# Gated linear attention and two expert layers: the chunk state packed, its product on a 2x2 grid of array tiles, the masked products one slot later

## The chip, the cores and the metric

One Trainium2 chip, one of its cores (NeuronCores). The metric is the device time of the whole program in microseconds (us), less is better. TensorE does the matrix products, VectorE (DVE) and ScalarE (ACT) the elementwise work, GpSimd (POOL) small fills and indirect transfers; SyncE (SP) issues nearly all DMA transfers, one after the other. Each engine takes its instructions in a fixed order that was settled when the kernel was built.

## What is computed

Three stages, cut to what matters. B = 4 batches, H = 8 heads, S = 768 steps, D = 48; 3072 tokens of width 384.

```
f = 1 / (1 + exp(-f_logit))
for t in range(S):
    state = f[:, :, t, :, None] * state + einsum('bhd,bhde->...', k[:, :, t], v[:, :, t])   # outer product k v
    y[:, :, t] = einsum('bhd,bhde->bhe', q[:, :, t], state)
x = y as tokens x (heads * D)
h = x @ w_in;  x2 = (h * sigmoid(h)) @ w_out                # d_ff 2048
expert = argmax(x2 @ w_gate) per token;  out = gate * relu(x2 @ w1[expert]) @ w2[expert]     # 8 experts
```

## The kernel before

**Tiling and stages.** The 3072 tokens are 24 chunks of 128 (six a batch, numbered n = 0 to 23), in groups of two or three chunks. For each chunk the attention runs as six stages, `att0` to `att5`: att0 turns f_logit into logarithms (Exp and Ln on ScalarE); att1 sums them along the chunk with a triangular matrix (`pl`), takes exponentials (`en`, `ep`), scales k and q (`kpad`, `qpad`, each head padded from 48 to 64 columns) and sends the last row of `ep` through DRAM (`ends`) into `a_all`, the factor by which the state decays over the chunk; att2 transposes q and k (`pq`, `pk`, copied to `qt`, `kt`: 112 rows hold a pair of heads, rows 0 to 47 one head, 64 to 111 the other); att3 makes the scores (`sc`, two row tiles of 64 rows) and masks them with the triangle on VectorE (`am`); att4 makes the products; att5 splits the result into two parts of fewer bits (`xth`, `xtl`) for the next layer.

**att4 in the chunks from n = 7 on (`turned`, n >= YT).** The result is kept transposed. `py` first takes the state's part: one matmul for each pair of heads, with a 112 x 112 block of `state` that holds the two heads' 48 x 48 states on its diagonal and zeros beside them, moving `qt`. Then eight matmuls `py<-am,v` add the chunk's own part, each with a head's v (48 columns) as weights; the two heads of a pair write partitions 0 to 47 and 64 to 111, which are two column tiles of the array. ScalarE copies `py` to `yt` (one copy of 112 x 512), and six DMA transfers bring the rows of `yt` into `y`, from where att5 reads. Then `pu` (eight matmuls, kpad as weights, v moving) gives the state's update, which VectorE adds to and scales in `state`: two operations for each of the two heads of a pair, on 48 partitions each. The first chunk of a batch has no state product, the last has no `pu`. In chunks 0 to 6 the result is not turned, and am is the weight.

**What sets the order.** The first expert layer runs beside this as a sequence of slots. A slot is one step of 128 columns of its hidden width for one group: `moe_h` (nine matmuls `ph<-xtl/xth,in_*`), `se` on ScalarE, `sg` on VectorE, `moe_g` (`gh` on ScalarE, `gl` on VectorE), and, two slots behind (LAG = 2), `moe_o` (nine matmuls `px<-out_*`). Each attention stage is hung on a slot: for chunks from 7 on, stage j of a chunk stands at s0 + S1[j], where s0 is ASH slots ahead of the chunk's place in the group before (spacing about five slots), and its loads stand four slots ahead of s0. Within a slot ph comes first, then the stages, then gh and gl, then px. TensorE's order is kept as written; a scheduler settles the places on the other engines and queues. Matmul results live in eight PSUM banks: two for ph (`h`), three for px (`x`), and three (`a`) in turn for everything of the attention and for the gate's small matmuls (`plt`, `pg`, `pr`).

**Names.** In the trace a tile's name stands without its number: `py<-am,v` is a product of masked scores. Each f32 matmul is two records, a matmul of the rounded parts (fp32r) is one. `out_again`, `in_again` and `wmin` belong to a second reading of the weights that is spread over the slots. L333 is the helper through which all matmuls go, L338 that of the transposes.

Of the kernel before, what the change touches and what calls it, by code (L numbers as in the profile page):

```python
# [9 lines left out]
F32 = mybir.dt.float32  # L10
# [6 lines left out]
ALU = mybir.AluOpType  # L17
# [4 lines left out]
P = 128  # L22
# [29 lines left out]
ST5 = (7, 10, 12, 16, 16, 18)  # L52
ST6 = (14, 17, 19, 21, 23, 25)
LD = (-30, -30, -10, -5, -3, 5, 11)
S1 = (-2, 1, 3, 5, 6, 8)
ASH = 3
SG = 2
SE = 2
GB = 3
# [28 lines left out]
YT = 7  # L88
# [5 lines left out]
def kernel(  # L94
# [43 lines left out]
    att = phase.enter_context(tc.tile_pool(name="att", bufs=1))  # L138
    late = phase.enter_context(tc.tile_pool(name="late", bufs=1))

    def bank(kind, name):
        return ps.tile([P, 512], F32, tag=kind, name=name, bufs={"h": 2, "x": 3, "a": 3}[kind])
# [12 lines left out]
    a_all = const.tile([P, NCH, NPR], F32, name="a_all")  # L155
    state = const.tile([P, (NPR - 1) * 112 + P], F32, name="state")
    state_of = [state[:, r * 112 : r * 112 + P] for r in range(NPR)]
    state_all = state[:, : NPR * 112].rearrange("p (r e) -> p r e", r=NPR)
    qpads = [const.tile([P, H, 64], F32, name=f"qpad{i}") for i in range(2)]
    kpads = [const.tile([P, H, 64], F32, name=f"kpad{i}") for i in range(2)]  # L160
    wgc = const.tile([P, KC, 32], F32, name="wgc")
# [6 lines left out]
    def use(n, i, name):  # L168
        return bank(BANKS.get(n, "aaaaaaaa")[i], name)

    loaded = {}
# [7 lines left out]
    def load_chunk(n, names):  # L179
        b, c = divmod(n, CPB)  # L180
        g, r = group_of[n]
        for nm in names:
            src = {"f": f_logit, "q": q, "k": k, "v": v}[nm]
            if n == 1:
                tag = {"f": "sg", "q": "gh", "k": "gh", "v": "gl"}[nm]
                t = att.tile([P, H, D], F32, tag=tag, name=f"{nm}_{n}", bufs=BUFS[tag])
            elif nm == "f":
                if n == 0 or n == starts[g] and g > 1:
                    fb[g] = att.tile([P, CPG, H, D], F32, tag="in_f", name=f"f_{n}")
                t = fb[g][:, r] if g > 1 else fb[0][:, max(n - 1, 0)]  # L190
            else:
                t = att.tile([P, H, D], F32, tag="in_" + nm, name=f"{nm}_{n}")
            nc.sync.dma_start(out=t, in_=src[b, :, c * P : (c + 1) * P, :].rearrange("h p d -> p h d"))
            loaded[nm, n] = t

    units = {}

# [110 lines left out]
    am = {}  # L308
    ysb = {}
# [97 lines left out]
    def att4(n):  # L407
        _, qt = bd.pop(n)
        vt = loaded.pop(("v", n))
        a = am.pop(n)  # L410
        first, last = n % CPB == 0, n % CPB == CPB - 1
        py = use(n, 5, f"py_{n}")
        turned = n >= YT
        for r in range(0 if first else NPR):
            if turned:
                pe.matmul(py[:112, r * P : (r + 1) * P], state_of[r][:112, :112], qt[:, r, :], start=r == 0, stop=False)
        for r in range(NPR):
            if not turned and not first:
                pe.matmul(
                    py[:, r * 2 * D : (r + 1) * 2 * D], qt[:, r, :],  # L420
                    state_of[r][:112].rearrange("p (j e) -> p j e", j=2)[:, :, :D], start=True, stop=False,
                )
            for j in range(2):
                h = 2 * r + j
                ah = a[j][:, r, :]
                if turned:
                    o = py[64 * j : 64 * j + D, r * P : (r + 1) * P]
                    pe.matmul(o, vt[:, h, :], ah, start=first and r == 0, stop=r == NPR - 1)
                else:
                    pe.matmul(py[:, h * D : (h + 1) * D], ah, vt[:, h, :], start=first, stop=first or j == 1)  # L430
        if turned:
            yt = att.tile([P, NPR, P], F32, tag="am", name=f"yt_{n}", bufs=2)
            for rows in ((slice(0, D), slice(64, 64 + D)) if first else (slice(0, 112),)):
                nc.scalar.copy(yt[rows], py[rows].rearrange("p (r t) -> p r t", r=NPR))
            y = att.tile([P, KC, P], F32, tag="y", name=f"y_{n}")
            for j in range(2):
                nc.sync.dma_start(out=y[j * D : (j + 1) * D], in_=yt[64 * j : 64 * j + D, :KC])
            for src, dst, c, m in ((0, 96, 0, 32), (32, 96, 1, 16), (64, 112, 1, 16), (80, 96, 2, 32)):
                nc.sync.dma_start(out=y[dst : dst + m, c], in_=yt[src : src + m, KC])
        else:  # L440
            y = att.tile([P, KC, P], F32, tag="y", name=f"y_{n}")
            nc.scalar.copy(y[:, :, :96], py[:, : KC * 96].rearrange("p (c f) -> p c f", c=KC))
            nc.scalar.copy(y[:, :, 96:], py[:, KC * 96 : DM].rearrange("p (c f) -> p c f", c=KC))
        ysb[n] = y
        if last:
            return
        pu = use(n, 6, f"pu_{n}")
        for r in range(NPR):
            for j in range(2):
                h = 2 * r + j  # L450
                pe.matmul(
                    pu[64 * j : 64 * j + D, r * D : (r + 1) * D], kpads[n % 2][:, h, :D], vt[:, h, :], start=True, stop=True
                )
        pu3 = pu[:112, : NPR * D].rearrange("p (r e) -> p r e", r=NPR)
        for j in range(2):
            rows, cols = slice(64 * j, 64 * j + D), slice(0, D)
            ab = a_all[rows, n, :, None].to_broadcast([D, NPR, D])
            s = state_all[rows, :, 64 * j : 64 * j + D]
            if first:
                nc.vector.tensor_tensor(out=s, in0=pu3[rows, :, cols], in1=ab, op=ALU.mult)  # L460
            else:
                nc.vector.tensor_tensor(out=s, in0=pu3[rows, :, cols], in1=s, op=ALU.add)
                nc.vector.tensor_tensor(out=s, in0=s, in1=ab, op=ALU.mult)

    def att5(n):
        g, r = group_of[n]
        if r == 0:
            xt[g] = xt0 if g == 0 else tuple(
                att.tile([P, CPG, KC, P], F32R, tag=f"xt{s}", name=f"xt{s}_{g}", bufs=2) for s in ("h", "l")
            )  # L470
        xh, xl = xt[g]
        y = ysb.pop(n)
        if n >= YT:
            nc.scalar.copy(xh[:, r], y)
            nc.vector.tensor_sub(xl[:, r], y, xh[:, r].bitcast(F32))
            return
        pt = use(n, 7, f"pt_{n}")
# [37 lines left out]
    def moe_o(g, i):  # L515
        hi, lo = gt.pop((g, i))
        first, last = (0,), (NF - 1,)
        wh, wl = units["out", i // 4]
        if i in first:
            px[g] = [bank("a" if (g, t) == (1, 1) else "x", f"px_{g}_{t}") for t in range(sizes[g])]  # L520
        for t in range(sizes[g]):
            o = px[g][t][:, :DM]
            m = slice(t * P, (t + 1) * P)
            pe.matmul(o, hi[:, m], wl[:, i % 4, :], start=i in first, stop=False)
            pe.matmul(o, lo[:, m], wh[:, i % 4, :], start=False, stop=False)
            pe.matmul(o, hi[:, m], wh[:, i % 4, :], start=False, stop=i in last)
        if i in last:
            moe_x2(g, i)
# [583 lines left out]
    for n in range(NCH):  # L1112
        g, r = group_of[n]
# [22 lines left out]
    for j in range(2 * NF):  # L1136
        s = VS + j * VD // 2
# [55 lines left out]
    first = min(plan)  # L1193
# [19 lines left out]
    def fill(n):  # L1213
        for fn, i in ops[:n]:
            fn(items["head"], i)
        del ops[:n]

    def preload():
# [4 lines left out]
        o=lambda: moe_o(*outs.pop(0)), f=lambda: fill(1), F=lambda: fill(len(ops)), l=lambda: logits_pe(g),  # L1223
        m=lambda: logits_pe2(g), p=lambda: pick(g), r=lambda: route(g), w=preload, k=rank_rest,
# [51 lines left out]
```

## Time and profile before

| | us |
|---|---|
| median of 3 runs (844.62 to 848.91) | 847.7 |
| profiled execution | 845.27 |
| its span, first to last instruction | 843.6 |
| TensorE busy in it | 810.5 (96%) |
| VectorE, ScalarE busy | 483.4 (57%), 377.1 (45%) |
| mean granted clock of TensorE | 0.989 of full |

The program has an early part up to about 140 us in which the weights arrive and the first seven chunks run, a middle part up to about 560 us in which the slots and the chunks run side by side, and the eight experts after that. Matmuls are pipelined: a record of TensorE lasts from its first column to its last result, so that records overlap, and the distance between two starts tells what one costs. Where the start of the next instruction is later than that, the row gives the idle time and the engine that ended it in brackets.

### The profile page before, as it was taken

The numbers are of one execution on the slowest core, as the hardware profiler recorded it, in microseconds if no ns is written. First come the engines' busy times: TensorE is split into PE (matmuls) and PEld (weight loads), VectorE is DVE, ScalarE is ACT, GpSimd is POOL, SyncE is SP. The second block draws the span as 40 slices with busy tenths as digits, with TensorE's granted clock in tenths as the row PEclk, the third lists the DMA queues.
The fourth block names the chain that finished last, engine by engine and source line by source line (L and its number), as shares of the span: only waits on it lengthen the run. The fifth ranks groups of instructions, "written<-read, shape, count | busy, mean of one in ns | idle before, by whom it ended". The sixth has DMA issues, their size and how long they took to land.

```text
span 843.6 us, 15324 instructions
## 1 busy us (share of the span) xinstructions
PE 810.5 (96%) x5692; PEld 766.8 (91%) x5692; DVE 483.4 (57%) x1293; ACT 377.1 (45%) x805; POOL 59.1 (7%) x94
## 2 busy tenths in 40 slices
PE   7799989999999999999999999999999999999994
PEld 4689889999999999999999999989999999999993
DVE  5999965566665556555666556366464526435520
ACT  4565464453453453444444333365273525435520
POOL 2000000002001001001001000001110010110001
PEclk9899999999999999999999999999999999999998
DMA  9856863313244343254343321342281615624500
GB/s 206 189 147 163 250 193 96 66 39 101 74 100 104 74 94 106 67 105 104 76 95 94 86 57 48 104 132 67 97 276 55 200 56 171 200 80 164 168 16 27
DMA packets 166435, 95.92 MB, mean 114 GB/s; under 512 B 115692, under 2 KB 159965, under 8 KB 166352
## 3 DMA queue, kind: packets, MB, share of 16 engines
q1 hardware_dynamic: 162224, 83.80, 37.5%
q0 software_dynamic: 3280, 9.49, 2.9%
q10 hardware_dynamic: 848, 1.57, 0.6%
q8 instruction: 46, 0.75, 0.4%
q14 instruction: 37, 0.30, 0.1%
HBM read 75.61 MB, written 16.33 MB: 109 GB/s over the span
## 4 chain that ended last, share of the span: by engine, by line
PE 60%; DMA 12%; issue 10%; DVE 9%; ACT 4%; SPq 3%; POOLq 0%; POOL 0%; DVEq 0%; ACTq 0%
PE px L333 19%; PE ph L333 18%; DMA out_dram<-o,oi 6%; PE py L333 4%; PE po L333 4%; PE p L333 4%; PE sc L333 2%; DMA w_raw<-in_moe_w_dram 1%; DMA f<-in_f_logit_dram 1%; DVE am L404 1%; PE pl L333 1%; PE p_r L333 1%; PE po_r L333 1%; PE pq L338 1%; PE pk L338 1%
## 5 line engine op out<-in xcount | busy, mean ns | idle before, releaser
L333 PE MATMUL px<-out_lo,gh 128*128 128x384 f32 x384 | 137.3, 357 | 0.3 <-ACT gh L511 0.3
L501 ACT ACTIVATE se<-ph 128x384 f32<-128x384 f32 (+1 forms) x144 | 65.3, 454 | 159.7 <-PE ph L333 157.1
L333 PE MATMUL px<-out_hi,gl 128*128 128x384 f32 x384 | 130.2, 339 | 2.2 <-DVE gl L512 2.2
L333 PE MATMUL px<-out_hi,gh 128*128 128x384 f32 x384 | 129.7, 338 | 0.0
L333 PE MATMUL ph<-xtl,in_hi 128*128 128x384 f32 (+1 forms) x384 | 125.5, 327 | 1.2 <-DVE sg L503 0.9
L503 DVE SCALAR_TENSOR_TENSOR sg<-se,ph 128x384 f32<-128x384 f32 (+1 forms) x144 | 73.0, 507 | 90.9 <-ACT se L501 89.0
L333 PE MATMUL ph<-xth,in_hi 128*128 128x384 f32 (+1 forms) x384 | 124.0, 323 | 0.0
L333 PE MATMUL ph<-xth,in_lo 128*128 128x384 f32 (+1 forms) x384 | 123.8, 322 | 0.0
L511 ACT CAST gh<-sg 128x384 fp32r<-128x384 f32 (+1 forms) x144 | 68.7, 477 | 70.5 <-DVE sg L503 61.5
L512 DVE TENSOR_TENSOR gl<-sg,gh 128x384 fp32r<-128x384 f32 (+1 forms) x144 | 73.4, 510 | 29.2 <-ACT gh L511 28.1
L333 PEld LDWEIGHTS ph<-xtl,in_hi 128*128 128x128 f32 x384 | 72.5, 189 | 3.8 <-issue 1.4
L333 PEld LDWEIGHTS px<-out_hi,gl 128*128 128x128 f32 x384 | 72.6, 189 | 3.6 <-DVE gl L512 3.2
L333 PEld LDWEIGHTS px<-out_lo,gh 128*128 128x128 f32 x384 | 72.4, 188 | 3.2 <-ACT gh L511 0.9
L333 PEld LDWEIGHTS ph<-xth,in_lo 128*128 128x128 f32 x384 | 72.5, 189 | 0.0
L333 PEld LDWEIGHTS ph<-xth,in_hi 128*128 128x128 f32 x384 | 72.4, 189 | 0.0
L333 PEld LDWEIGHTS px<-out_hi,gh 128*128 128x128 f32 x384 | 72.3, 188 | 0.0
L227 DVE TENSOR_TENSOR w_lo<-w_raw,w_hi 128x384 fp32r<-128x384 f32 x128 | 65.1, 552 | 12.5 <-ACT w_hi L226 11.8
L333 PE MATMUL po<-w_lo,hh 128*128 128x384 f32 (+6 forms) x200 | 67.8, 339 | 0.0
L333 PE MATMUL po<-w_hi,hh 128*128 128x384 f32 (+6 forms) x200 | 67.2, 336 | 0.0
L333 PE MATMUL po<-w_hi,hl 128*128 128x384 f32 (+6 forms) x200 | 67.2, 336 | 0.0
L226 ACT CAST w_hi<-w_raw 128x384 fp32r<-128x384 f32 x124 | 56.9, 513 | 22.8 <-DMA w_raw<-in_moe_w_dram 19.5
L333 PE MATMUL p<-xsl,w_hi 128*128 128x480 f32 (+6 forms) x168 | 58.5, 348 | 0.0
(243 smaller groups left out, 1437.9 us busy)
## 6 DMA issues: line engine op xcount, KB each, us to landing
w_raw<-in_moe_w_dram SPq DMA_DIRECT2D x64, 384.0 KB
xs<-big SPq DMA_DIRECT2D x8, 776.0 KB
out_again<-in_moe_w_out_dram SPq DMA_DIRECT2D x16, 384.0 KB
xe<-xs SPq DMA_DIRECT2D x7, 776.0 KB
out_raw<-in_moe_w_out_dram SPq DMA_DIRECT2D x13, 384.0 KB
f<-in_f_logit_dram SPq DMA_DIRECT2D x24, 192.0 KB
k<-in_k_dram SPq DMA_DIRECT2D x24, 192.0 KB
q<-in_q_dram SPq DMA_DIRECT2D x24, 192.0 KB
```

What stands on the lines that cost most here:

```text
L226: (keep(nc.scalar.copy) if key == ("w1", 1, 1) and RT > 1 else nc.scalar.copy)(hi[:, h], x)
L227: lo_engine.tensor_sub(lo[:, h], x, hi[:, h].bitcast(F32))
L333: ins = nc.tensor.matmul(*a, **k)
L338: ins = nc.tensor.transpose(*a, **k)
L404: nc.vector.tensor_tensor(out=a, in0=sc4, in1=tri4, op=ALU.mult)
L501: nc.scalar.activation(e, ph[:, :GT], AF.Tanh, scale=0.5)
L503: nc.vector.scalar_tensor_tensor(out=t, in0=e, scalar=1.0, in1=ph[:, :GT], op0=ALU.add, op1=ALU.mult)
L511: (nc.scalar.copy if g < GACT else nc.vector.tensor_copy)(hi, t)
L512: (nc.gpsimd if (g, i) < LOV else nc.vector).tensor_sub(lo, t, hi.bitcast(F32))
```

## The change

Three things are changed, all of them in the attention.

1. **The state is packed.** From chunk 6 on each pair of heads takes 64 columns of `state` and not 112: the 48 x 48 state of one head on partitions 0 to 47, that of the other on 64 to 111, in the same columns. `carry` updates both with one add and one scaling on 112 partitions, where there were two of each on 48. For this `pu` is written 64 rows high for each head (kpad with its padding as weights).
2. **The state product is by head.** `att4_turned` makes eight matmuls of 48 rows and 64 columns, on the four tiles of a 2x2 grid of the array; the result goes to two banks, `pya` and `pyb`, of which the second has the two heads of a pair with partitions exchanged. The products of v and am go to the same places, with 64 columns of v as weights (v gets 16 columns more behind the last head, filled with zeros by GpSimd). `pu` follows in the columns of `pya` that are left. ScalarE copies the two banks in two halves, and y is brought into place by eight transfers and not six. 
3. **The slots.** ASH goes from 3 to 4 and the last two entries of S1 from 6 and 8 to 7 and 9: for chunks from 7 on, loads and att0 to att3 come a slot earlier, att4 and att5 stay where they were.

```
-S1 = (-2, 1, 3, 5, 6, 8)
-ASH = 3
+S1 = (-2, 1, 3, 5, 7, 9)
+ASH = 4
...
+    packed_state = state[:, : NPR * 64].rearrange("p (r e) -> p r e", r=NPR)
...
+            if nm == "v":
+                tag, bufs = ("gl", GB) if n == 1 else ("in_v", 1)
+                flat = att.tile([P, H * D + 16], F32, tag=tag, name=f"v_{n}", bufs=bufs)
+                if n >= YT:
+                    nc.gpsimd.memset(flat[:, H * D :], 0.0)
...
+        if turned:
+            att4_turned(n, qt, vt, a, first, last)
+            return
         py = use(n, 5, f"py_{n}")
-        turned = n >= YT
-        for r in range(0 if first else NPR):
-            if turned:
-                pe.matmul(py[:112, r * P : (r + 1) * P], state_of[r][:112, :112], qt[:, r, :], start=r == 0, stop=False)
...
-                if turned:
-                    o = py[64 * j : 64 * j + D, r * P : (r + 1) * P]
-                    pe.matmul(o, vt[:, h, :], ah, start=first and r == 0, stop=r == NPR - 1)
...
-            for j in range(2):
-                nc.sync.dma_start(out=y[j * D : (j + 1) * D], in_=yt[64 * j : 64 * j + D, :KC])
-            for src, dst, c, m in ((0, 96, 0, 32), (32, 96, 1, 16), (64, 112, 1, 16), (80, 96, 2, 32)):
-                nc.sync.dma_start(out=y[dst : dst + m, c], in_=yt[src : src + m, KC])
...
+        packed = n >= CPB
+        wide = 64 if packed else D
         for r in range(NPR):
             for j in range(2):
                 h = 2 * r + j
                 pe.matmul(
-                    pu[64 * j : 64 * j + D, r * D : (r + 1) * D], kpads[n % 2][:, h, :D], vt[:, h, :], start=True, stop=True
+                    pu[64 * j : 64 * j + wide, r * D : (r + 1) * D], kpads[n % 2][:, h, :wide],
+                    vt[:, h * D : (h + 1) * D], start=True, stop=True,
                 )
+        if packed:
+            carry(n, pu[:112, : NPR * D], first)
+            return
...
+    def carry(n, pu, first):
+        pu3 = pu.rearrange("p (r e) -> p r e", r=NPR)
+        ab = a_all[:112, n, :, None].to_broadcast([112, NPR, D])
+        s = packed_state[:112, :, :D]
+        if first:
+            nc.vector.tensor_tensor(out=s, in0=pu3, in1=ab, op=ALU.mult)
+        else:
+            nc.vector.tensor_tensor(out=s, in0=pu3, in1=s, op=ALU.add)
+            nc.vector.tensor_tensor(out=s, in0=s, in1=ab, op=ALU.mult)
+
+    def att4_turned(n, qt, vt, a, first, last):
+        halves_of = [use(n, 5, f"pya_{n}"), use(n, 6, f"pyb_{n}")]
+
+        def place(r, j):
+            b, c = divmod(r, 2)
+            k = j ^ b
+            return halves_of[b][64 * k : 64 * k + 64, c * P : (c + 1) * P]
+
+        if not first:
+            for c in range(2):
+                for r in (c, c + 2):
+                    for j in range(2):
+                        rows = slice(64 * j, 64 * j + D)
+                        pe.matmul(place(r, j), packed_state[rows, r, :], qt[rows, r, :], start=c == 0, stop=False)
+        for r in range(NPR):
+            for j in range(2):
+                h = 2 * r + j
+                pe.matmul(
+                    place(r, j), vt[:, h * D : h * D + 64], a[j][:, r, :], start=first and r % 2 == 0, stop=r % 2 == 1
+                )
+        pu = halves_of[0][:, 2 * P : 2 * P + NPR * D]
+        if not last:
...
+                    pe.matmul(
+                        pu[64 * j : 64 * j + 64, r * D : (r + 1) * D], kpads[n % 2][:, h, :],
+                        vt[:, h * D : (h + 1) * D], start=True, stop=True,
+                    )
+        yt = att.tile([P, NPR, P], F32, tag="am", name=f"yt_{n}", bufs=2)
+        for b in range(2):
+            nc.scalar.copy(
+                yt[:112, 2 * b : 2 * b + 2], halves_of[b][:112, : 2 * P].rearrange("p (r t) -> p r t", r=2)
+            )
+        y = att.tile([P, KC, P], F32, tag="y", name=f"y_{n}")
+        for j in range(2):
+            nc.sync.dma_start(out=y[j * D : (j + 1) * D, :2], in_=yt[64 * j : 64 * j + D, :2])
+            nc.sync.dma_start(out=y[j * D : (j + 1) * D, 2], in_=yt[64 - 64 * j : 64 - 64 * j + D, 2])
+        for src, dst, c, m in ((64, 96, 0, 32), (96, 96, 1, 16), (0, 112, 1, 16), (16, 96, 2, 32)):
+            nc.sync.dma_start(out=y[dst : dst + m, c], in_=yt[src : src + m, KC])
```

Up to the slot in which chunk 7's scans start, TensorE's order is the same but for the width of chunk 6's pu. Three places where it is not follow; x4 is a row that repeats, sizes are those of the result.

TensorE at the products of chunk 8, before:

```order
L333 MATMUL ph_8_2207<-xth_1059,in_hi 128x384
L333 MATMUL py_2221<-qt_2084,state 112x128 x4
L333 MATMUL py_2221<-am_0_2170,v_1810 48x128
L333 MATMUL py_2221<-am_1_2172,v_1810 48x128
...
L333 MATMUL pu_2243<-v_1810,kpad_88 48x48 x8
L333 MATMUL pl_2256<-lfh_2087,trir 128x384
L333 MATMUL pl_2256<-lfl_2088,trir 128x384
L338 MATMUL plt_1_2268<-ident,x_1_1867 128x128 x3
L333 MATMUL px_0_1930<-out_lo,gh_6_2131 128x384
```

The four rows of the state product are eight after it, and pl of the next chunk has gone a slot ahead:

```order
L341 MATMUL ph_8_2226<-xth_1059,in_hi 128x384
L341 MATMUL pya_2240<-qt_2054,state 64x128 x2
L341 MATMUL pyb_2241<-qt_2054,state 64x128 x2
L341 MATMUL pya_2240<-qt_2054,state 64x128 x2
L341 MATMUL pyb_2241<-qt_2054,state 64x128 x2
L341 MATMUL pya_2240<-am_0_2148,v_1784 64x128
...
L341 MATMUL pyb_2241<-am_0_2148,v_1784 64x128
...
L341 MATMUL pya_2240<-v_1784,kpad_88 64x48 x8
L346 MATMUL plt_1_2288<-ident,x_1_1868 128x128 x3
L341 MATMUL px_0_1947<-out_lo,gh_6_2152 128x384
```

VectorE at the masks of chunk 17 (am; sg and gl are the expert layer's, wmin waits for a transfer of weights), before:

```order
L503 SCALAR_TENSOR_TENSOR sg_7_4686<-se_7_4684,ph_7_4674 128x384
L260 TENSOR_REDUCE wmin<-out_again 128x1
L404 TENSOR_TENSOR am_0_4698<-sc_0_4688,trir 128x512
L404 TENSOR_TENSOR am_1_4700<-sc_1_4689,trir 128x512
L512 TENSOR_TENSOR gl_7_4703<-sg_7_4686,gh_7_4702 128x384
L503 SCALAR_TENSOR_TENSOR sg_8_4727<-se_8_4725,ph_8_4715 128x384
```

After it the masks stand ahead of gl_6 and of that wmin, and sg_7 behind both:

```order
L412 TENSOR_TENSOR am_0_4712<-sc_0_4702,trir 128x512
L713 TENSOR_REDUCE r_lim_4924<-r_oh_4724 128x3
L731 COPY x_12_4461<-r_den_4730 128x1
L412 TENSOR_TENSOR am_1_4714<-sc_1_4703,trir 128x512
L568 TENSOR_TENSOR gl_6_4736<-sg_6_4700,gh_6_4735 128x384
L714 TENSOR_TENSOR r_off_4734<-r_off_4734,r_lim_4924 128x3
L715 TENSOR_SCALAR r_lim_4924<-r_lim_4924 128x3
L268 TENSOR_REDUCE wmin<-out_again 128x1
L334 CAST lfh_4920<-f_4831 128x384
L559 SCALAR_TENSOR_TENSOR sg_7_4760<-se_7_4758,ph_7_4748 128x384
```

ScalarE at the end of the middle part, where xth of chunk 23 waits for y, before:

```order
L434 COPY yt_6493<-py_6480 112x512
L501 ACTIVATE se_12_6540<-ph_12_6530 128x384
L511 CAST gh_12_6544<-sg_12_6542 128x384
L474 CAST xth_6206<-y_6495 128x384
L501 ACTIVATE se_13_6567<-ph_13_6557 128x384
L511 CAST gh_13_6579<-sg_13_6569 128x384
```

After it there are two copies to yt, and xth stands behind se_13:

```order
L508 COPY yt_6592<-pya_6574 112x256
L508 COPY yt_6592<-pyb_6575 112x256
L557 ACTIVATE se_12_6642<-ph_12_6632 128x384
L567 CAST gh_12_6646<-sg_12_6644 128x384
L557 ACTIVATE se_13_6669<-ph_13_6659 128x384
L530 CAST xth_6300<-y_6595 128x384
L567 CAST gh_13_6681<-sg_13_6671 128x384
```

So ScalarE's wait for y there now has gh_13 right behind it, and no longer se_13.

## Rows read from the trace of the kernel before

**Rows 1.** Busy time by stretch: window, length, busy us of each engine, clock, DMA.

```profile
140.00:530.00 390.00, 388.53 (x2939) 371.34 (x2938) 231.07 (x658) 169.15 (x335) 18.88 (x19) 1.00 0.34 83
```

**Rows 2.** What TensorE waited for, 140 to 545 us: total, times, longest.

```profile
PE py L333 <- DVE am L404: 1.4, 5, 0.6
PE ph L333 <- DVE sg L503: 0.9, 1, 0.9
```

**Rows 3.** Timeline of TensorE, chunk 7's products: start, length, what, count.

```profile
151.52 0.34 PE L333 MATMUL ph<-xth,in_hi 128*128 128x384 f32 x1
151.69 1.04 PE L333 MATMUL py<-qt,state 112*112 112x128 f32 x8
152.66 1.08 PE L333 MATMUL py<-am,v 128*48 128x128 f32 x16
153.57 0.53 PE L333 MATMUL pu<-v,kpad 128*48 128x48 f32 x16
154.03 0.44 PE L333 MATMUL pl<-lfh,trir 128*128 128x384 f32 x1
```

**Rows 4.** Timeline of TensorE, chunk 7's scores.

```profile
147.09 0.34 PE L333 MATMUL ph<-xth,in_hi 128*128 128x384 f32 x1
147.36 1.16 PE L333 MATMUL sc<-qt,kt 48*128 48x128 f32 x16
148.45 0.44 PE L333 MATMUL px<-out_lo,gh 128*128 128x384 f32 x1
```

**Rows 5.** Timeline of TensorE, one group's gate products.

```profile
229.81 0.86 PE L333 MATMUL pg<-rt,wgc 128*32 128x128 f32 x18
```

**Rows 6.** Timeline of TensorE, chunk 6: am as weights, then pu.

```profile
118.58 1.88 PE L333 MATMUL py<-v,am 128*128 128x48 f32 x16
120.39 0.56 PE L333 MATMUL pu<-v,kpad 128*48 128x48 f32 x16
```

**Rows 7.** Timeline of TensorE, products of chunks 11, 14, 17 and 23, and what followed.

```profile
243.97 1.04 PE L333 MATMUL py<-qt,state 112*112 112x128 f32 x8
...
247.18 0.44 PE L333 MATMUL pl<-lfh,trir 128*128 128x384 f32 x1
...
311.62 1.04 PE L333 MATMUL py<-qt,state 112*112 112x128 f32 x8
...
314.41 0.44 PE L333 MATMUL pl<-lfh,trir 128*128 128x384 f32 x1
...
379.47 1.04 PE L333 MATMUL py<-qt,state 112*112 112x128 f32 x8
...
382.38 0.44 PE L333 MATMUL pl<-lfh,trir 128*128 128x384 f32 x1
...
524.16 1.04 PE L333 MATMUL py<-qt,state 112*112 112x128 f32 x8
...
526.14 0.44 PE L333 MATMUL px<-out_lo,gh 128*128 128x384 f32 x1
```

**Rows 8.** Timeline of VectorE ahead of chunk 17's masks.

```profile
379.57 0.55 DVE L260 TENSOR_REDUCE wmin<-out_again 128x1 f32<-128x384 f32 x1 [1.19 <-DMA out_again<-in_moe_w_out_dram]
```

**Rows 9.** Groups by form: count, busy us, mean ns of one, idle before.

```profile
L434 ACT COPY yt<-py 112x512 f32<-112x512 f32 x15 | 8.8, 584 | 2.6 <-PE py L333 2.4
L462 DVE TENSOR_TENSOR state<-pu,state 48x192 f32<-48x192 f32 x24 | 8.5, 354 | 0.4
```

**Rows 10.** ScalarE's wait for y; SyncE's issues of y, chunk 7.

```profile
ACT xth L474 <- DMA y<-yt: 18.6, 17, 5.4
...
154.62 1.25 SPq L437 DMA_DIRECT2D y<-yt  x2
155.91 2.49 SPq L439 DMA_DIRECT2D y<-yt  x4
```

**Rows 11.** Timeline of ScalarE and TensorE where chunk 23's y comes late.

```profile
536.65 0.51 ACT L474 CAST xth<-y 128x384 fp32r<-128x384 f32 x1 [5.38 <-DMA y<-yt]
...
538.28 0.45 PE L333 MATMUL ph<-xtl,in_hi 128*128 128x384 f32 x1 [0.87 <-DVE sg L503]
```

More of the change, by code (lines that the diff above doesn't have):

```diff
@@ L183, in load_chunk @@
             src = {"f": f_logit, "q": q, "k": k, "v": v}[nm]
-            if n == 1:
-                tag = {"f": "sg", "q": "gh", "k": "gh", "v": "gl"}[nm]
+            if nm == "v":
[3 more added lines that the diff above has]
+                    nc.gpsimd.memset(flat[:, H * D :], 0.0)
+                t = flat[:, : H * D].rearrange("p (h d) -> p h d", h=H)
+                loaded[nm, n] = flat
+            elif n == 1:
+                tag = {"f": "sg", "q": "gh", "k": "gh"}[nm]
                 t = att.tile([P, H, D], F32, tag=tag, name=f"{nm}_{n}", bufs=BUFS[tag])
@@ L193, in load_chunk @@
             nc.sync.dma_start(out=t, in_=src[b, :, c * P : (c + 1) * P, :].rearrange("h p d -> p h d"))
-            loaded[nm, n] = t
+            loaded.setdefault((nm, n), t)
     units = {}
@@ L411, in att4 @@
         first, last = n % CPB == 0, n % CPB == CPB - 1
+        turned = n >= YT
+        if turned:
+            att4_turned(n, qt, vt, a, first, last)
+            return
         py = use(n, 5, f"py_{n}")
-        turned = n >= YT
-        for r in range(0 if first else NPR):
-            if turned:
-                pe.matmul(py[:112, r * P : (r + 1) * P], state_of[r][:112, :112], qt[:, r, :], start=r == 0, stop=False)
         for r in range(NPR):
-            if not turned and not first:
+            if not first:
                 pe.matmul(
@@ L424, in att4 @@
                 h = 2 * r + j
-                ah = a[j][:, r, :]
-                if turned:
-                    o = py[64 * j : 64 * j + D, r * P : (r + 1) * P]
-                    pe.matmul(o, vt[:, h, :], ah, start=first and r == 0, stop=r == NPR - 1)
[L429 to L435, printed above, removed]
-            for j in range(2):
-                nc.sync.dma_start(out=y[j * D : (j + 1) * D], in_=yt[64 * j : 64 * j + D, :KC])
-            for src, dst, c, m in ((0, 96, 0, 32), (32, 96, 1, 16), (64, 112, 1, 16), (80, 96, 2, 32)):
-                nc.sync.dma_start(out=y[dst : dst + m, c], in_=yt[src : src + m, KC])
[L440 to L443, printed above, removed]
+                pe.matmul(
+                    py[:, h * D : (h + 1) * D], a[j][:, r, :], vt[:, h * D : (h + 1) * D], start=first,
+                    stop=first or j == 1,
+                )
+        y = att.tile([P, KC, P], F32, tag="y", name=f"y_{n}")
+        nc.scalar.copy(y[:, :, :96], py[:, : KC * 96].rearrange("p (c f) -> p c f", c=KC))
+        nc.scalar.copy(y[:, :, 96:], py[:, KC * 96 : DM].rearrange("p (c f) -> p c f", c=KC))
         ysb[n] = y
@@ new lines, in att4_turned @@
+    def att4_turned(n, qt, vt, a, first, last):
[4 more added lines that the diff above has]
+            return halves_of[b][64 * k : 64 * k + 64, c * P : (c + 1) * P]
+        if not first:
+            for c in range(2):
[11 more added lines that the diff above has]
+        if not last:
+            for r in range(NPR):
+                for j in range(2):
+                    h = 2 * r + j
+                    pe.matmul(
+                        pu[64 * j : 64 * j + 64, r * D : (r + 1) * D], kpads[n % 2][:, h, :],
[5 more added lines that the diff above has]
+                yt[:112, 2 * b : 2 * b + 2], halves_of[b][:112, : 2 * P].rearrange("p (r t) -> p r t", r=2)
+            )
+        y = att.tile([P, KC, P], F32, tag="y", name=f"y_{n}")
+        for j in range(2):
+            nc.sync.dma_start(out=y[j * D : (j + 1) * D, :2], in_=yt[64 * j : 64 * j + D, :2])
+            nc.sync.dma_start(out=y[j * D : (j + 1) * D, 2], in_=yt[64 - 64 * j : 64 - 64 * j + D, 2])
+        for src, dst, c, m in ((64, 96, 0, 32), (96, 96, 1, 16), (0, 112, 1, 16), (16, 96, 2, 32)):
+            nc.sync.dma_start(out=y[dst : dst + m, c], in_=yt[src : src + m, KC])
+        ysb[n] = y
+        if not last:
+            carry(n, pu[:112], first)
```

## Prediction

> **What bounds the kernel now.** I read the busy time by stretch first. Between 140 and 530 us, the stretch that holds the products of all 17 chunks that the change treats anew (7 to 23), TensorE is busy 388.5 of 390 us at a granted clock of 1.00 [rows 1]. The list of what TensorE waits for in 140 to 545 us has two lines: masks (am) from VectorE, 1.4 us of idle in five waits, and one 0.9 us wait for a sg [rows 2]. So nothing but TensorE's own stream and those waits sets the end there; a microsecond taken out of the stream, or out of these waits, comes off the whole, and work on ScalarE and VectorE counts only where it makes TensorE late. I then read one changed chunk (chunk 7) record by record on TensorE [rows 3], the scores (sc) that feed its masks [rows 4], and the chunks whose products had to wait [rows 7].
>
> In [rows 3] the state product is 8 records (each f32 matmul is two) that follow one another: 152.66 - 151.69 = 0.97 us to the first am product, of which 0.10 is the change of tiling between them (next part); the rest is 0.11 us a step. From the start of the last ph before it to the first am product it takes 152.66 - 151.52 = 1.14 us. The am products and pu are 16 records each, but in two column tiles side by side: 0.91 us and 0.46 us for 8 steps.
>
> **The state product on a 2x2 grid: 15 chunks (7 to 11, 13 to 17, 19 to 23).** It becomes 16 records, by head, with 48 rows and 64 columns, 4 for each of four tiles. No row of before has such tiles, so I bound them. The nearest is sc [rows 4]: 16 records in two row tiles, 128 columns moving. Its first record stands 147.36 - 147.09 = 0.27 us after the last ph, against 151.69 - 151.52 = 0.17 for the state product now: that is the price of one more change of tiling, 0.10 us. From its first record to the next px, change of tiling included, it takes 1.09 us for 8 steps. With four tiles at work at once there are 4 steps: 1.09 - 4 x 0.11 = 0.65. The weights are 64 columns wide and not 128: the am products, with 48, last 1.08 us from first start to last end where sc lasts 1.16 [rows 3, 4], so up to 0.06 less. New block: 0.27 + 0.59 to 0.65 = 0.86 to 0.92, for 1.14: a saving of 0.22 to 0.28 us. I take 0.25; 15 x 0.25 = **3.8 us less**. That three tiles can run at once shows in the gate's 18 records, 6 for each of three column tiles, that last 0.86 us [rows 5]; in single file they would need 18 x 0.11 = 2.0.
>
> **Wider weights.** The stationary slice grows from 48 to 64 columns in the am products and in pu. The am products move 128 columns, which take the 0.11 step with any width of weights seen here, so nothing changes. pu moves only 48. With 48 moving columns behind 128 columns of weights, chunk 6 needs (120.39 - 118.58)/16 = 0.113 us a record; behind 48 columns chunk 7's pu needs (154.03 - 153.57)/8 = 0.057 a step [rows 3, 6]. Between these, 64 columns cost 16/80 x 0.056 = 0.011 more a step, 0.09 for 8 steps; there are 15 such pu (6 to 10, 12 to 16, 18 to 22; the last chunk of a batch has none): **1.3 us more**. Bounds: 0 (48 moving columns hide it) and 1.6.
>
> **Products one slot later.** Relative to the rest of the program the scans, transposes, scores and masks come one slot of 16 earlier; the products and xth stay. So the masks have two slots and not one. Four chunks paid for this. Chunk 11 took 247.18 - 243.97 = 3.21 us from first product to the next matmul, chunk 17 382.38 - 379.47 = 2.91, where chunk 23, without wait and also without pu, took 526.14 - 524.16 = 1.98; chunk 14 took 314.41 - 311.62 = 2.79, chunk 7 154.03 - 151.69 = 2.34 [rows 3, 7]. That is 1.23 + 0.93 + 0.45 = 2.6 us (the list of waits counts less, since a column tile that waits beside one that runs is not idle time there). Why they wait: chunk 17's masks stood on VectorE behind a wmin that waited 1.19 us for the landing of out_again [rows 8]; in the new order they stand ahead of it. **2.6 us less**; bounds 1.3 (half stay) and 3.0 (chunk 18 waited a little too).
>
> **What lies beside TensorE.** The carry is two VectorE operations and not four of 0.35 us [rows 9]: 0.7 us less a chunk, not on the path. The yt copy of 0.58 us [rows 9] becomes two of half the width, together under 1.2 us. The second must be over before the carry may read the same bank, a new wait on VectorE, behind which sg, kpad and gl are queued. Nothing of this reaches TensorE unless it grows past about 3 us: the bank that a sg frees is needed when the ph after next starts, two px blocks and one ph later, 27 steps of some 0.17 us [rows 3], of which se and sg themselves take about 1. The small POOL memsets of v have five slots.
>
> The y transfers become 8 and not 6. Each holds SyncE's queue 0.62 us ((1.25 + 2.49)/6), so y lands 1.25 us later. ScalarE already waits at xth, 18.6 us over 17 chunks, at longest 5.4 [rows 10], with se, gh and qt queued behind. The longest one shows what the cover is worth: ScalarE idled 5.38 us and TensorE 0.87 [rows 11], so some 4.5 us are free. The other sixteen wait (18.6 - 5.4)/16 = 0.83 us on average; 0.83 + 1.25 = 2.1 stays within 4.5. For chunk 23 xth now stands behind se_13, so that ph_15 no longer waits, but gh_13 and gl_13 do, and px_13 needs them: between 0.9 less and 1.3 more; I take 0.
>
> **Sum:** -3.8 + 1.3 - 2.6 = -5.1 us. On the profiled execution, 845.27 us (span 843.6, the rest lies around it), this gives 840.2. That execution lies 2.4 us under the median of the three runs, 847.7; a term that is a time of TensorE's stream is the same on either, so the forecast for the median is 842.6.
>
> **The rivals.**
> *Pairs.* Two row tiles write the two halves of one bank here, which no row of before shows: sc's two row tiles have a bank each, and the column tiles that share one have the same rows. If such writes exclude one another, the grid runs two at a time, 8 steps: 0.89 + 4 x 0.11 = 1.33 us, 0.19 more than now. 15 x 0.19 = 2.9; 2.9 + 1.3 - 2.6 = +1.6: 849.3 us. For it: nothing measured; against it: each pair writes disjoint partitions, as the column tiles do. The Trainium skill has the rule that speaks for it ("TensorEngine Tiling (Array Packing)", Gotcha 1: PSUM Pressure): different row tiles cannot access the same PSUM bank at the same time, and by it the time would be these 849.3 us. Its page "PSUM — Partial Sum Buffer" (PSUM bank collisions raise a hardware error) narrows that to one bank and 32-partition quadrant and says that the chip does not stall for it; no run here shows either.
> *Single file.* The four tiles don't overlap at all, since a head's records alternate over rows and columns: 16 steps, 0.89 + 12 x 0.11 = 2.21 us, 1.07 more; 15 x 1.07 = 16.1, + 1.3 - 2.6 = +14.8: 862.5, slower. This decides from the point where a block takes over 1.14 + (4.2 + 1.3)/15 = 1.51 us, ten steps. For it: the change of tiling costs time already in [rows 3]; against it: rows 4 and 5, where tiles of one direction overlap fully.
> *Masks still late.* VectorE's in-order queue puts something else ahead of the masks and the 2.6 us stay: 845.2. For it: wmin waits for a landing wherever it stands; against it: the new order.
> *y too late.* If two more transfers delay y by 5 us, as where the queue was crowded at the end, 0.83 + 5 - 4.5 = 1.3 us at 17 chunks, 23 us: 865. For it: [rows 11]; against it: the sixteen others.
>
> **How the numbers follow.** The forecast, with cover and bounds as above (840 to 845 us): 0.60. Pairs: 0.11. Single file: 0.06. Masks still late: 0.13. y too late: 0.05. Something else: 0.05. Half a per cent is 4.2 us, about what a measurement of this kernel can tell from no change; the forecast's -5.1 lies close to that line, so that of its 0.60 I put 0.46 beyond it and 0.14 within; masks still late gives 0.02 and 0.11, pairs 0.10 within and 0.01 slower, single file and y too late are slower, the rest is split. Faster 0.50, same 0.36, slower 0.14. The range holds the forecast, late masks and most of pairs: down to 838.5 (0.28 for each block, 3.0 of waits, pu for nothing, 0.9 at the end: -8.1, and a little), up to 849.5.
>
> **What would show it.** In the profile after, chunk 7's state records (pya, pyb from qt) should start in fours within some 0.03 us, and last start of ph to first am product should read 0.9 us; 1.3 means pairs, 2.2 single file. pu should last 0.09 us longer. The mask waits should be gone from TensorE's list, xth's idle time should be 1 to 1.3 us longer at those chunks where it stands at the same place in ScalarE's queue, with no new line for sg or gl on TensorE. If TensorE waits for gl or sg at more than one or two chunks, the reasoning on the cover is wrong.

## The result: 859.6 us, slower by 1.5%

| | before | after |
|---|---|---|
| median of 4 runs, taken in turn | 846.6 us (844.6 to 848.9) | 859.6 us (858.3 to 861.8) |
| ratio, 95% interval | | 1.0146 [1.0123, 1.0169] |
| profiled execution, and its span | 845.27, 843.6 us | 858.32, 856.3 us |

The forecast was 842.6 us with a range that ended at 849.5. The products of the change did what was forecast, and the time was lost elsewhere. First the list of what TensorE waited for from 140 to 545 us in the kernel after (total, times, longest), which answers to [rows 2]:

```profile
PE pg L341 <- ACT rt L633: 6.4, 4, 3.0
PE pg L341 <- ACT qt L392: 2.3, 1, 2.3
PE ph L341 <- DVE xtl L531: 1.0, 1, 1.0
PE ph L341 <- DVE sg L559: 0.2, 1, 0.2
```

The waits for masks (am) are gone, as forecast. In their place stand 9.9 us of waits, of which 8.7 belong to products that the prediction never looked at: pg, the gate's small matmuls, waiting for ScalarE. Now chunk 7 on TensorE, which answers to [rows 3]:

```profile
154.90 0.34 PE L341 MATMUL ph<-xth,in_hi 128*128 128x384 f32 x1
155.16 0.33 PE L341 MATMUL pya<-qt,state 48*64 48x128 f32 x2
155.18 0.33 PE L341 MATMUL pyb<-qt,state 48*64 48x128 f32 x2
155.32 0.28 PE L341 MATMUL pya<-qt,state 48*64 48x128 f32 x2
...
155.54 0.28 PE L341 MATMUL pya<-qt,state 48*64 48x128 f32 x2
155.56 0.28 PE L341 MATMUL pyb<-qt,state 48*64 48x128 f32 x2
155.76 0.66 PE L341 MATMUL pya<-am,v 128*64 128x128 f32 x8
156.25 0.61 PE L341 MATMUL pyb<-am,v 128*64 128x128 f32 x8
156.69 0.62 PE L341 MATMUL pya<-v,kpad 128*64 128x48 f32 x16
157.24 0.44 PE L341 MATMUL px<-out_lo,gh 128*128 128x384 f32 x1
```

The state records start in fours, the last start of ph lies 155.76 - 154.90 = 0.86 us ahead of the first am product (1.14 before), pu takes 157.24 - 156.69 = 0.55 us (0.46 before), and the whole block 157.24 - 154.90 = 2.34 us where chunk 7 took 154.03 - 151.52 = 2.51: 0.17 less, as the two terms 0.25 and 0.09 say together.

**Where pg waits.** TensorE and ScalarE of the kernel after, where group 1's gate falls:

```profile
170.19 0.84 PE L341 MATMUL pg<-rt,wgc 128*32 128x128 f32 x10 [2.97 <-ACT rt L633]
```

```profile
161.58 1.17 ACT L326 ACTIVATE f<-f 128x1152 f32<-128x1152 f32 x1 [0.35 <-DMA v<-in_v_dram]
...
163.65 1.28 ACT L327 ACT_TABLE_LOAD   x1
164.94 1.17 ACT L327 ACTIVATE f<-f 128x1152 f32<-128x1152 f32 x1
166.02 0.46 ACT L633 COPY rt<-plt 128x384 f32<-128x384 f32 x1
167.46 0.51 ACT L530 CAST xth<-y 128x384 fp32r<-128x384 f32 x1 [0.98 <-DMA y<-yt]
167.98 1.28 ACT L557 ACT_TABLE_LOAD   x1
169.28 0.49 ACT L557 ACTIVATE se<-ph 128x384 f32<-128x384 f32 x1
169.66 0.47 ACT L633 COPY rt<-plt 128x384 f32<-128x384 f32 x1
```

pg multiplies the copies rt. ScalarE runs in order, and Exp and Ln of f (the first stage of the next group's three chunks) with the load of a function table (ACT_TABLE_LOAD) behind each, 1.17 + 1.28 + 1.17 + 1.28 = 4.9 us, now stand ahead of the second copy, and all but the last load ahead of the first. In the kernel before the two copies were out first and f came after them:

```profile
158.26 0.47 ACT L577 COPY rt<-plt 128x384 f32<-128x384 f32 x1
...
163.47 0.47 ACT L577 COPY rt<-plt 128x384 f32<-128x384 f32 x1
...
167.23 1.17 ACT L318 ACTIVATE f<-f 128x1152 f32<-128x1152 f32 x1
```

At this wait the idle TensorE is paid twice, since its granted clock falls behind it; behind the waits of 2.14 us at 376.75 and 2.32 us at 444.93 it stayed at 1.00. Busy time by stretch, kernel after (window, length, busy us of PE, PEld, DVE, ACT, POOL, then granted clock, DMA share, GB/s):

```profile
165.00:170.00 5.00, 2.22 (x14) 1.70 (x12) 0.76 (x2) 3.99 (x6) 0.00 (x0) 1.00 0.03 9
170.00:175.00 5.00, 4.81 (x31) 4.17 (x33) 1.26 (x3) 1.40 (x4) 0.00 (x0) 0.66 0.00 0
```

The clock is 1.00 (2.4 GHz) until the stall and 0.66 on average after it, so it stood at 1.2 GHz for part of that stretch; 0.34 x 5 = 1.7 us of work at the full clock.

**Ledger.** Starts of the first ph of slots 16, 128 and 136, read from the timelines, cut the span in four; the later tables use the same cuts.

| us | to slot 16 | 16 to 128 | 128 to 136 | 136 to the end | span |
|---|---|---|---|---|---|
| before | 88.8 | 452.7 | 20.8 | 281.3 | 843.6 |
| after | 91.7 | 460.1 | 23.0 | 281.5 | 856.3 |

From slot 16 to 128 the kernel is 7.4 us longer: 15 blocks save 15 x 0.17 = 2.6, the waits of before (1.4 + 0.9) go, 9.9 us of waits and 1.7 of clock come: +6.7, most of the 7.4. The 2.2 us of slots 128 to 136 are told at the end. The 2.9 us ahead of slot 16 go with TensorE's clock in the ramp up, and neither half of the change sets them by itself. From 25 to 30 and 30 to 35 us it was 0.69 and 0.96 before, 0.50 and 0.54 after; but grid_act (below), which has the grid, had 0.72 and 0.94, and slots_gate_late, which lacks it, 0.50 and 0.57. The clock in these ten microseconds is not all of it, either: gate_late, which comes to slot 16 at 91.1 us, has 0.89 and 0.77 there, and its first pk, at 14.41 us where the kernel before has 12.50, is late already. So up to 3 us of any two profiled spans here mean nothing, and the ratios of medians decide. Each stretch in the tables comes from one execution, so it shows where time goes, and not to the last microsecond how much.

### The profile page after: what moved, and what is told of

It reads as the page before. It is cut to its first block, busy times and chain, and to the rows that moved or that the text cites. A ratio compares the mean times of both kernels' runs of the same rounds, so it can differ in the third digit from the quotient of the medians.

```text
span 856.3 us, 15611 instructions
## 1 busy us (share of the span) xinstructions
PE 817.5 (95%) x5812; PEld 767.7 (90%) x5812; DVE 470.9 (55%) x1266; ACT 376.8 (44%) x820; POOL 61.2 (7%) x111
## 4 chain that ended last, share of the span: by engine, by line
PE 49%; DMA 18%; issue 16%; DVE 9%; ACT 4%; SPq 3%; POOLq 0%; POOL 0%; ACTq 0%; DVEq 0%
PE ph L341 19%; PE px L341 17%; DMA out_dram<-o,oi 10%; PE pya L341 2%; PE sc L341 2%; DMA f<-in_f_logit_dram 2%; DMA y<-yt 1%; PE py L341 1%; DMA out_dram<-o_r,oi_r 1%; PE pl L341 1%; DVE w_lo L235 1%; SPq L516 1%; DVE sg L559 1%; DMA in_again<-in_moe_w_in_dram 1%; DVE gl L568 1%
## 5 line engine op out<-in xcount | busy, mean ns | idle before, releaser
L235 DVE TENSOR_TENSOR w_lo<-w_raw,w_hi 128x384 fp32r<-128x384 f32 x128 | 65.2, 554 | 12.4 <-ACT w_hi L234 11.6
```

Of the source, the lines that this page charges most:

```text
L235: lo_engine.tensor_sub(lo[:, h], x, hi[:, h].bitcast(F32))
```

## The experiments

Theory 1: with the earlier scans, f's Exp and Ln stand ahead of the gate's copies on ScalarE. Theory 2: the eight transfers of y instead of six make SyncE's queue, and with it f and y, late. Ratios are to the kernel before, run in turn on the same chip.

**One half each: grid_only and slots_only.** grid_only is the kernel after with

```diff
-S1 = (-2, 1, 3, 5, 7, 9)
-ASH = 4
+S1 = (-2, 1, 3, 5, 6, 8)
+ASH = 3
```

> The packed state, the 2x2 grid and its transfers stay; the slots are those of before (first stage 5 slots ahead of the old position, masked products in their old slot). Theory 1 (the earlier scans put the Exp and Ln of f ahead of the gate's copies on ScalarE): the waits of the gate's products on ScalarE for 2 to 3 us go, the waits for the masks (about 1.4 us at five chunks) come back, and the time is that of before less the grid's gain of some 2.5 us: 844, between 841 and 848. Theory 2 (the eight transfers of the turned y make the queue of SyncE late, and f and y with it): those waits stay, and the time stays over 853.

slots_only is the kernel before with the same lines the other way round.

> The kernel before with the slots of the change and nothing else: products and transfers of y as before. Theory 1 (order on ScalarE): the gate's products wait for ScalarE as in the changed kernel, and the time is 855, between 850 and 862, although the waits for the masks go. Theory 2 (transfers of y): no such waits; the masks' waits go, 844, between 841 and 847.

| | median us | ratio, 95% interval | to slot 16 | 16 to 128 | 128 to 136 | to the end |
|---|---|---|---|---|---|---|
| grid_only | 848.3 | 0.999 [0.997, 1.001] | 91.1 | 450.7 | 22.6 | 281.9 |
| slots_only | 858.5 | 1.011 [1.009, 1.014] | 88.9 | 464.1 | 21.1 | 280.8 |

The slots alone make the kernel before slower by 1.1%; the grid alone is level with it (844 had been expected), 2.0 us better in its own stretch (16 to 128) and 1.9 worse in the next. So the slots are the loss. In slots_only, which has the transfers of before, TensorE waited for:

```profile
PE pg L333 <- ACT rt L577: 3.1, 1, 3.1
PE pg L338 <- ACT rt L591: 2.8, 2, 2.0
PE ph L333 <- DVE sg L503: 2.1, 1, 2.1
PE pg L333 <- ACT qt L384: 1.7, 1, 1.7
```

Theory 2 fell as the cause of the whole loss. It was not empty, though. In grid_only, with the slots of before, the masks' waits (1.5 us) have company:

```profile
PE ph L341 <- DVE xtl L531: 2.5, 3, 1.6
PE pya L341 <- DVE am L412: 1.5, 2, 1.4
```

xtl is the low half of y's cast, and ph reads it at once. ScalarE's and TensorE's rows of the longest of these waits in grid_only:

```profile
210.60 0.51 ACT L530 CAST xth<-y 128x384 fp32r<-128x384 f32 x1 [3.91 <-DMA y<-yt]
```

```profile
211.76 0.45 PE L341 MATMUL ph<-xtl,in_hi 128*128 128x384 f32 x1 [1.55 <-DVE xtl L531]
```

ScalarE waited 3.91 us for y and TensorE 1.55: the cover of a late y is here 3.91 - 1.55 = 2.4 us, not the 4.5 of the prediction. ScalarE's wait for y in all: 29.4 us in grid_only, 31.0 after, 18.6 before [rows 10].

**Stages put back: scan_back and masks_early.** The kernel after with the first two stages (f; the scan), or the first three, in the slots of before:

```diff
-S1 = (-2, 1, 3, 5, 7, 9)
+S1 = (-1, 2, 3, 5, 7, 9)   scan_back
+S1 = (-1, 2, 4, 5, 7, 9)   masks_early
```

> The changed kernel with its first two stages (f's Exp and Ln, the scan's product) put back in the slots of before; the scores' and masks' stages stay one slot earlier, and the grid and the transfers stay. Theory 1 (order on ScalarE): the Exp and Ln of f stand behind the gate's copies again, the gate's waits of 2 to 3 us go, the masks are still early: 842, between 839 and 846, which would be the forecast of the whole change. Theory 2 (transfers of y): 853 or more.

> The changed kernel with its first three stages put back in the slots of before, so that only the masks' stage stands one slot earlier against the products; the grid stays. Theory 1 (order on ScalarE): 843, between 840 and 848; the transposed q and the scores now lie one slot apart, so that a wait of the scores for the copy of q on ScalarE may cost 1 to 3 us against the kernel with two stages back. Theory 2 (transfers of y): 853 or more.

Both came out against theory 1 as I had put it: scan_back 858.5 us, 1.012 [1.009, 1.015]; masks_early 853.9 us, 1.007 [1.003, 1.011]. The long waits for rt did shrink to one of 1.6 and one of 2.1 us, but others came up. scan_back:

```profile
PE pq L346 <- DVE qpad L365: 8.6, 6, 2.7
PE pg L341 <- ACT rt L633: 1.6, 1, 1.6
```

With scan and transposes one slot apart, the padded q, which VectorE makes from the scan's result, is late six times. masks_early has 3.9 us of waits for xtl, 2.1 for rt and 1.0 for kt. What is left there of the waits for rt is not f's doing: the second copy stands behind a cast that waits for y, 2.38 us here and 2.30 in scan_back:

```profile
168.66 0.51 ACT L530 CAST xth<-y 128x384 fp32r<-128x384 f32 x1 [2.38 <-DMA y<-yt]
...
169.49 0.47 ACT L633 COPY rt<-plt 128x384 f32<-128x384 f32 x1
```

So the two kernels do not tell "f behind the copies" from "f ahead of them", and both times lie where theory 2 had put them (853 or more): scan_back brings a wait of its own, since scan and transposes stand only one slot apart, and in masks_early most of the waits go back to y. The question had to be put without touching the stages.

**The gate given more cover: gate_late, slots_gate_late, rt_on_vector.** The first two move pg and what follows it one slot later for all groups but the last two, in the kernel after and in slots_only:

```diff
-        at_end(s0 - 1, gate, g)
-        at_end(s0, gate_rows, g)
-        s0 += 1
+        gl8 = 1 if g < NG - 2 else 0
+        at_end(s0 - 1 + gl8, gate, g)
+        at_end(s0 + gl8, gate_rows, g)
+        s0 += 1 + gl8
```

> The changed kernel with the gate's small products pg and what follows them (down to the choice of the experts) one slot later, about 4.3 us, for all groups but the last two; the copies rt stay in their order on ScalarE, behind the Exp and Ln of f. Theory 1 (the gate waits for copies that stand behind f's Exp and Ln): the four waits of pg, 8.7 us in the profile of the changed kernel, and the lower clock after the first of them, 1.7 us of work at full clock between 170 and 175 us, go: 849, between 846 and 853. Theory 2 (the eight transfers of the turned y): little change, 857 to 861, since the late y and f stay late.

> The kernel of slots_only (products and transfers of before, slots of the change) with the gate's products and what follows them one slot later. Theory 1: the waits of pg (7.6 us in the profile of slots_only) and the lower clock after them (5 us of work between 165 and 175 and 440 and 450 us) go: 847, between 844 and 851. A rival, that the earlier scans delay VectorE or ScalarE for all users and the gate is only where it shows: 854 or more, with new waits at other products.

The third is the kernel after with the copies off ScalarE's queue:

```diff
-        nc.scalar.copy(rt.rearrange("p c t -> p (c t)"), pt[:, :DM])
+        nc.vector.tensor_copy(rt.rearrange("p c t -> p (c t)"), pt[:, :DM])
```

> The changed kernel with the copies rt of the gate's rows on VectorE, out of ScalarE's queue; slots, gate, grid and transfers as changed. Theory 1 (the gate waits because its copies stand behind f's Exp and Ln on ScalarE): the waits of pg for rt go, the gate stays where it is, 852, between 848 and 856; the waits for xtl stay. A rival (the gate's rows themselves come late, or any queue would do it): pg waits as long for VectorE, 857 or more.

| | median us | ratio, 95% interval | 16 to 128 | 128 to 136 |
|---|---|---|---|---|
| after | 859.6 | 1.015 [1.012, 1.017] | 460.1 | 23.0 |
| gate_late | 851.5 | 1.002 [1.000, 1.004] | 456.8 | 22.5 |
| rt_on_vector | 851.6 | 1.004 [1.003, 1.005] | 453.0 | 22.8 |
| slots_only | 858.5 | 1.011 [1.009, 1.014] | 464.1 | 21.1 |
| slots_gate_late | 848.2 | 0.999 [0.997, 1.000] | 453.4 | 21.1 |

Two different edits, one that leaves the copies where they are and gives pg a slot more, and one that takes them out of ScalarE's queue, win back most of the loss: by the ratios, 1.28% and 1.06% of 847 us, 10.8 and 9.0 of 12.4 us. In slots_only the first edit wins back all of it. Theory 1 stands in this form: with the earlier scans the copies rt no longer reach the gate in time on ScalarE. (The later gate was not run in the kernel before, but there is no wait of pg in [rows 2] for it to win. gate_late's profiled execution took 853.7 us, 2.2 more than its median, with a stall of 2.64 us for xtl that ends at 282.09 us and a clock of 0.65 from 280 to 285 us and 0.67 from 285 to 290, so its stretch reads longer than its median says. rt_on_vector keeps 3.8 us of waits of pg, now for VectorE.)

What is left shows why the waits for masks brought nothing when they went. gate_late:

```profile
PE ph L341 <- DVE xtl L531: 4.4, 3, 2.6
PE pl L341 <- DVE am L412: 1.5, 1, 1.5
```

and slots_gate_late has the second of these too (2.2 us), the rows of VectorE and of TensorE:

```profile
312.05 0.55 DVE L260 TENSOR_REDUCE wmin<-in_again 128x1 f32<-128x384 f32 x1 [2.54 <-DMA in_again<-in_moe_w_in_dram]
312.52 0.54 DVE L503 SCALAR_TENSOR_TENSOR sg<-se,ph 128x384 f32<-128x384 f32 x1
312.98 1.28 DVE L404 TENSOR_TENSOR am<-sc,trir 128x512 f32<-128x512 f32 x2
```

```profile
313.72 0.44 PE L333 MATMUL pl<-lfh,trir 128*128 128x384 f32 x1 [2.23 <-DVE am L404]
```

It is the wait of [rows 8] again, a wmin for the landing of a weight block, with masks behind it. The products no longer wait for these masks, but the next scan (pl) does: the masks release what it writes to. From slot 16 to 128 slots_gate_late needs 453.4 us and the kernel before 452.7: early masks were worth nothing there. This one landing took most of what they could give: 2.23 us of wait, and a granted clock of 0.92 from 310 to 315 us and 0.74 from 315 to 320, 1.7 us more.

**The transfers off SyncE's queue.** In grid_only and in gate_late, the four small ones of the eight transfers of y are issued from another queue (nc.gpsimd or nc.scalar in place of nc.sync in the last dma_start of att4_turned).

> The kernel of grid_only with the four small transfers of the turned y on GpSimd's queue. If the three waits for xtl in grid_only (1.6, 0.5 and 0.4 us, none in the kernel before) come of SyncE's longer queue, they go: 846, between 844 and 848, faster than grid_only. If they come of the transfers themselves, however issued, they stay or grow: 848 to 851.

> The kernel of gate_late with the four small transfers of the turned y issued on GpSimd's queue, so that SyncE issues four for each chunk. If the transfers cost on top of the gate's waits, the waits for xtl go too (1.0 us in the profile of the changed kernel, 2.5 us in that of grid_only): 846, between 843 and 850. If they cost nothing: as gate_late.

> The kernel of grid_only with the four small transfers on ScalarE's queue. If SyncE's queue is what costs (grid_pool: 397.2 us in the stretch from slot 32 to 128 against 399.8 in grid_only, with 7 us lost at the program's end): 846, between 844 and 848, and no waits for xtl. If ScalarE pays for the issues: 850 to 856.

> The kernel of gate_late with the four small transfers of the turned y issued on ScalarE's queue, behind the copies yt that they read. In gate_late_pool the stretch from slot 32 to slot 128 of the expert-free part took 395.5 us (before 401.9, gate_late 405.0), and 7 us went at the program's end. If the gain there comes of taking the small transfers out of SyncE's queue, it stays (395 to 398 us) and the end is as before: 846, between 842 and 849. If ScalarE pays for the four issues (about 0.5 us each, 2 us of its queue in each chunk, ahead of se and gh), the products wait for sg or gh: 850 to 858.

| | median us | ratio, 95% interval | to slot 16 | 16 to 128 | 128 to 136 | to the end |
|---|---|---|---|---|---|---|
| grid_pool | 852.7 | 1.005 [1.002, 1.007] | 91.5 | 448.1 | 23.0 | 287.6 |
| gate_late_pool | 852.2 | 1.003 [1.001, 1.005] | 91.2 | 447.6 | 22.7 | 289.8 |
| grid_act | 846.8 | 0.999 [0.997, 1.001] | 89.2 | 450.4 | 22.2 | 282.1 |
| gate_late_act | 852.8 | 1.006 [1.004, 1.007] | 91.5 | 457.2 | 22.7 | 282.3 |

On GpSimd's queue the waits for xtl are gone, and ScalarE waits 10.1 us for y in grid_pool instead of 29.4. From slot 16 to 128 gate_late_pool then takes 5.1 us less than the kernel before, which is the size of the forecast gain, with a wait of pl of 1.8 us left. So theory 2 holds for 2 to 3 us without the slots (450.7 - 448.1 = 2.6 between grid_only and grid_pool), and for more with them: between gate_late and gate_late_pool it is 456.8 - 447.6 = 9.2, of which 4.4 are waits for xtl and 3.4 the lower clock that comes with the longest of these. By the ratios gate_late_pool is 0.12%, 1.0 us, over gate_late, though its part from slot 136 on is 289.8 - 281.6 = 8.2 longer, so some 7 us is an estimate that does not hang on the stretch of one execution. But the end grows by 6.3 and 8.5 us (below), and the net is a loss.

On ScalarE's queue the end stays as it was; grid_act is level with before, while gate_late_act, where ScalarE's order is tighter, loses 0.6%. TensorE's longest wait there falls where ScalarE issues transfers:

```profile
230.39 3.53 ACTq L516 DMA_DIRECT2D y<-yt  x2
233.96 0.48 ACT L633 COPY rt<-plt 128x384 f32<-128x384 f32 x1 [6.17 <-DMA y<-yt]
```

Two issues held ScalarE for 3.5 us and the copy rt behind them, and TensorE waited 3.6 us for kt at 234.9 us. But kt is VectorE's, and there a wmin ahead of it had waited 3.75 us for a landing (until 232.32), so how much of the loss the issues make is not shown. Last, the gate a slot later in grid_act, as the candidate to be faster than both kernels:

> The kernel of grid_act with the gate's products and what follows them one slot later. grid_act keeps one wait of pg for rt (1.4 us at 182 us of its profile), with the slots of before. If the gate's cover is short there too, the wait goes: 845.5, between 843 and 848, a ratio to the kernel before of 0.996 to 0.999. If moving the gate only hands the wait to the next product, as with the waits for xtl and pl in gate_late: 847 or more, a ratio of 1.000 or more.

It gave 849.1 us, 1.001 [1.000, 1.003]: the wait of pg went and one of plt for am of 3.5 us came at 176.7 us. The second reading held. No kernel of the study is measurably faster than the kernel before.

## Why the prediction was wrong

- **The grid: right.** -0.25 a block was forecast, and 1.14 - 0.86 = 0.28 was measured; with pu, 0.17 net. The rivals pairs and single file fell: all four tiles run at once, though two row tiles write into one bank. The rule of the Trainium skill ("TensorEngine Tiling (Array Packing)", Gotcha 1: PSUM Pressure) that different row tiles cannot access one bank at a time shows in no cost here. grid_only fits the sum: 2.0 us better from slot 16 to 128, with 2.5 us of xtl waits already in it.
- **pu: right.** 0.09 us longer.
- **Masks: the mechanism half right, the term wrong.** The products stopped waiting, as forecast. But the 2.6 us were not won: a landing that VectorE waits for delays whatever stands behind it in its queue, and with the masks earlier that was the next scan. slots_gate_late puts the term at about 0 by its stretch and at 1.0 us by its ratio (0 to 2.5 by the interval), where I had 1.3 to 3.0.
- **"What lies beside TensorE": the step that failed.** Two mistakes. First, I followed the operations that the new text adds (yt, carry, y) and not all that the slots move: f's loads, its maximum, and Exp and Ln with their table loads moved too. The copies rt stood ahead of Exp and Ln on ScalarE and stand behind them now, and pg waits for these copies. I put at nothing what costs 9.0 us alone in slots_only (858.5, with 849.5 for the kernel before beside it), and the cover of 27 steps that I gave was that of sg. Second, I took the cover of a late y (4.5 us) from one place at the end, where sg was what came late. In the other slots the first reader is ph by way of xtl, whose cover in grid_only was 2.4 us, and the average wait that I had worked out myself, 2.1, leaves nothing for the longer ones. That is the rival "y too late", which I had at 23 us or nothing; it costs 2 to 3 without the slots and some 7 with them, in waits of ph and in copies rt that stand behind a waiting xth.
- **What would show it** named gl and sg as the lines to look for. The condition was met in spirit only: the new line was pg.

## To carry to other kernels

When a table moves a stage by a slot, list on each in-order engine every instruction that the stage issues and who now stands behind it; the cost falls there, often on a chain that the edit does not name. Cover belongs to one chain from one releaser to one matmul, so read it for each reader and at the tightest place. A wait for a landing in an in-order queue does not go away when its victim is moved: the next instruction behind it is the next victim.

## What the runs showed of the hardware

**A transfer whose last part lands late.** In all kernels with the grid, slots 128 to 136 take 1.3 to 2.3 us more than before. There gl waits behind a cast of xe_h, a transfer issued at 553.88 us before and 554.20 in grid_only. VectorE before, then in grid_only:

```profile
558.47 0.21 DVE L787 CAST oi_h<-xe_h 128x1 int32<-128x1 f32 x2 [1.19 <-DMA xe_h<-xs]
```

```profile
560.65 0.22 DVE L843 CAST oi_h<-xe_h 128x1 int32<-128x1 f32 x2 [3.07 <-DMA xe_h<-xs]
```

Busy time by stretch, before and then grid_only (the last two columns are the DMA share of 16 engines and GB/s):

```profile
557.00:558.00 1.00, 1.00 (x10) 0.97 (x9) 0.28 (x1) 0.91 (x3) 0.00 (x0) 1.00 0.79 293
558.00:559.00 1.00, 1.00 (x9) 1.00 (x9) 0.53 (x4) 1.00 (x4) 0.00 (x0) 1.00 0.01 2
```

```profile
557.00:558.00 1.00, 1.00 (x9) 0.97 (x9) 0.42 (x1) 0.75 (x3) 0.00 (x0) 1.00 0.98 363
558.00:559.00 1.00, 1.00 (x10) 1.00 (x9) 0.00 (x0) 1.00 (x3) 0.00 (x0) 1.00 0.19 64
559.00:560.00 1.00, 1.00 (x9) 1.00 (x8) 0.00 (x0) 0.71 (x3) 0.00 (x0) 1.00 0.06 23
```

The bulk has landed soon after 558.0 us in both, but in grid_only a share of 0.06, as much as one engine of 16, works on until about 560. This takes the grid's 2.0 us back in grid_only. No run tests why, but the packets in the traces point to a cause. On the queue that the profile lists as "q8 instruction", one packet of 16 KB runs while this transfer does (556.7 to 557.9 us in grid_only) in all eleven kernels with the grid, and the cast follows 5.9 to 6.6 us after the issue; in the three without the grid it ends 1.6 us or more ahead of the issue (551.3 to 552.3 before), and the cast follows after 4.6 to 4.9.

**Transfers issued by GpSimd lengthen the end.** The last scatter is issued at 836.21 us in grid_only and its span ends at 846.4, 10.2 later; in grid_pool it is issued at 833.53, and the span ends at 850.2, 16.7 later:

```profile
836.21 0.95 POOL L844 DMA_INDIRECT out_dram<-o,oi  x1 [4.25 <-DMA out_dram<-o,oi]
```

```profile
833.53 0.95 POOL L844 DMA_INDIRECT out_dram<-o,oi  x1 [4.51 <-DMA out_dram<-o,oi]
```

No engine works in the difference. The two kernels differ only in the queue that issues 68 small transfers, the last of them some 300 us earlier; gate_late_pool shows the same, 16.9 against 10.0 in gate_late. What the end waits for is not in the profile.
